# A gate in two TensorE passes: 2E copied by ScalarE, the difference taken by VectorE, the sum by POOL

## The chip, the cores and the metric

One core of one Trainium2 chip. The metric is the device time of one launch in microseconds; lower is better. A run of a kernel is several executions, of which one is recorded by the hardware profiler.

## The reference, cut to what matters

The real part of a two-dimensional Fourier transform over eight batches of 3008 x 256, and behind it a feed-forward layer with a gelu gate.

```python
def _attn_ref(x):                      # x: (8, 3008, 256)
    X = np.fft.fft(x, axis=1)
    X = np.fft.fft(X, axis=2)
    return X.real.astype(np.float32)

def _moe_ref(x, w_gate, w_val, w_out): # x: (24064, 256), d_ff = 1536
    g = x @ w_gate
    inv_sqrt2 = np.float32(1.0 / np.sqrt(2.0))
    gelu = 0.5 * g * (1.0 + erf(g * inv_sqrt2))
    val = x @ w_val
    return (gelu * val @ w_out).astype(np.float32)
```

## The kernel before

The transform of a real input is symmetric, so the kernel makes an even part E and an odd part O of the tokens and gets two tokens from each column: a token and its mirror. A batch is worked off in 36 blocks of 128 hidden units by 512, 512 or 481 columns (three chunks of twelve blocks). The text calls a block's place in the batch its slot, 0 to 35. `psum` gives banks of PSUM, into which all matmuls of this kernel write: two for the gate, three for the value, one for the output (ps_o) and two for the Fourier matmuls ("gate bank", "value bank" and "output bank" below).

```python
    def gelu_tile():
        return work([128, 2, TOK], BF16, "gelu", 5, "gelu_sb")
    def ve_tile():
        return work([128, TOK], FP32, "ve", 3, "ve_sb")
    def v_tile():
        return work([128, TOK], FP32, "v", 4, "v_sb")
    def psum(tag):
        bufs = {"g": 2, "v": 3, "o": 1, "dft": 2}[tag]
        return psum_pool.tile([128, 512], FP32, tag=tag, bufs=bufs, name=f"ps_{tag}")
```

The gate of a block is an E pass and an O pass into one bank, a gelu, then (one slot later) a pass with the weights -2O into the same bank and a second gelu for the mirror tokens. The value needs two passes only, because VectorE and POOL make the mirror:

```python
        def l1_gate(ci, fc):
            def run():
                n, _, E, O, st, fs = cols_of(ci, fc)
                pg = psum("g")
                mm(pg, n, "g", "E", fs, E, True, False)
                mm(pg, n, "g", "O", fs, O, False, True)
                gl = gelu_tile()
                nc.scalar.activation(gl[:, 0, :n], pg[:, :n], AF.Gelu)          # L676
                st["ps"][fc] = [pg, gl]
            return run
        def l1_gate2(ci, fc):
            def run():
                n, _, _, O, st, fs = cols_of(ci, fc)
                pg, gl = st["ps"][fc][:2]
                mm(pg, n, "g", "M", fs, O, False, True, skip_group_check=True)  # -2O
                nc.scalar.activation(_sub(gl, [[-1, n]], TOK + n - 1), pg[:, :n], AF.Gelu)  # L685
            return run
        # ... l1_value: E pass, then on VectorE
                nc.vector.scalar_tensor_tensor(                                 # L704
                    ve[:, :n], EB_bufs[b][:, c0 : c0 + n], yw[:, fc : fc + 1], pv[:, :n],
                    op0=ALU.mult, op1=ALU.add)
        # ... l1_value2: O pass, then
                nc.vector.tensor_tensor(st["h"][:, fc, 0, :n], gl[:, 0, :n], pv[:, :n], op=ALU.mult)   # L720
                vv = v_tile()
                nc.vector.scalar_tensor_tensor(                                 # L722
                    _sub(vv, [[-1, n]], n - 1), ve[:, :n], 2.0, pv[:, :n], op0=ALU.mult, op1=ALU.subtract)
                nc.gpsimd.tensor_tensor(st["h"][:, fc, 1, :n], gl[:, 1, :n], vv[:, :n], op=ALU.mult)   # L724
```

The changed kernel is called after below. POOL's folds are the sums and differences from which the next batch's E and O are made. In one slot the order is:

```python
            parts["G"][fc]()                      # gate of this block
            if before:
                before[0]["g"][before[1]]()       # -2O pass and second gelu of the block before
            parts["V"][fc]()                      # value E pass
            if len(two) == 2:
                two.pop(0)()                      # four output matmuls (L749)
            for f in pool.pop(i, []):
                f()                               # POOL's folds for the next batch
            if before:
                before[0]["v"][before[1]]()       # value O pass and products of the block before
            if two:
                two.pop(0)()                      # four output matmuls; some slots end with the copy of ps_o (L769)
            for f in fill.pop(i, []):
                f()                               # Fourier matmuls for the next batch
```

Of the kernel before, what the change touches and what calls it, by code (L numbers as in the profile page):

```python
# [9 lines left out]
FP32 = mybir.dt.float32  # L10
BF16 = mybir.dt.bfloat16
AF = mybir.ActivationFunctionType
ALU = mybir.AluOpType
# [5 lines left out]
def _sub(base: bass.AP, free_pattern, free_offset, part_start=0, part_num=None):  # L19
    p_step, p_count = base.ap[0]  # L20
    if part_num is None:
        part_num = p_count - part_start
    pat = [[p_step, part_num]] + [list(x) for x in free_pattern]
    off = base.offset + part_start * p_step + free_offset
    return ap_replace(base, ap=pat, offset=off)
# [3 lines left out]
def kernel(  # L29
# [8 lines left out]
    nc = tc.nc  # L38
# [5 lines left out]
    B, T, C = x.shape  # L44
# [6 lines left out]
    NFC = F // 128  # L51
# [33 lines left out]
    def work(shape, dt, tag, bufs, name):  # L85
        return work_pool.tile(shape, dt, tag=tag, bufs=bufs, name=name)
# [41 lines left out]
    def gelu_tile():  # L128
        return work([128, 2, TOK], BF16, "gelu", 5, "gelu_sb")
# [4 lines left out]
    def v_tile():  # L134
        return work([128, TOK], FP32, "v", 4, "v_sb")

    def osb_tile():
        return work([128, 2, C], FP32, "osb", 3, "out_sb")

# [3 lines that stand above are left out]
# [100 lines left out]
    keep2 = const_pool.tile([128, 1], FP32)  # L243
    dump = const_pool.tile([1, 1], FP32)
    one_h = const_pool.tile([1, 1], BF16)
    yw = const_pool.tile([128, NFC], FP32)
    NGP = NJ * NK
    ff = work([128, 2 * NGP], FP32, "EO", 2, "ff")
    rr = work([128, 2 * NGP], FP32, "EO", 2, "rr")
# [218 lines left out]
    def make_yw(f0, n):  # L468
# [7 lines left out]
            nc.scalar.activation(yw[:, c0 : c0 + nq], ps[:, 0:nq], AF.Copy)  # L476
        return run


    EO_bufs, EB_bufs = {}, {}  # L480
    turn = [0]
# [152 lines left out]
        return tp_e(b, gi, 1, engine)  # L634


    def store(b, gi, sub, sign, osb_half, queue):
        segs = [c for c in cols[gi] if c[0] // 128 == sub]
        m = min(128, chunk_len[gi] - sub * 128)
        for i, (off, k2, w) in enumerate(segs):  # L640
            p0 = off - sub * 128
            lo, hi = (1, w - 1) if sign and k2 == 0 else (0, w)
            if sign:
                t0 = T - k2 - N2 * (hi - 1)
                p1 = m - p0 - hi
            else:
                t0 = k2 + N2 * lo
                p1 = p0 + lo
            dst = ap_replace(
                out,  # L650
                ap=[[N2 * C, hi - lo], [1, C]],
                offset=out.offset + (b * T + t0) * C,
            )
            (nc.sync if i else queue).dma_start(out=dst, in_=_sub(osb_half, [[1, C]], 0, part_start=p1, part_num=hi - lo))

    def ffn_work(b):
        cstate = {}

        def mm(ps, n, nm, part, fs, src, start, stop, **kw):
            nc.tensor.matmul(ps[:, :n], W[nm, part][:, fs], src, start=start, stop=stop, **kw)  # L660

        def cols_of(ci, fc):
# [3 lines left out]
                cstate[ci] = {"h": h_tile(), "ps": {}, "pso": {}}  # L666
            return n, c0, E, O, cstate[ci], slice(fc * 128, (fc + 1) * 128)

        def l1_gate(ci, fc):
            def run():  # L670
                n, _, E, O, st, fs = cols_of(ci, fc)
                pg = psum("g")
                mm(pg, n, "g", "E", fs, E, True, False)
                mm(pg, n, "g", "O", fs, O, False, True)
                gl = gelu_tile()
                nc.scalar.activation(gl[:, 0, :n], pg[:, :n], AF.Gelu)  # L676
                st["ps"][fc] = [pg, gl]
            return run

        def l1_gate2(ci, fc):  # L680
            def run():
                n, _, _, O, st, fs = cols_of(ci, fc)
                pg, gl = st["ps"][fc][:2]
                mm(pg, n, "g", "M", fs, O, False, True, skip_group_check=True)
                nc.scalar.activation(_sub(gl, [[-1, n]], TOK + n - 1), pg[:, :n], AF.Gelu)  # L685
            return run
# [88 lines left out]
        for ci in range(NG):  # L775
            nsub = (chunk_len[ci] + 127) // 128
            parts = {k: [f(ci, fc) for fc in range(NFC)] for k, f in (
                ("G", l1_gate), ("V", l1_value), ("g", l1_gate2), ("v", l1_value2))}
            subs = [nsub - 1, *range(nsub - 1)] if last(ci) else range(nsub)
            l2s = [l2_piece(ci, s, g, f) for s in subs for g in range(2) for f in range(0, NFC, L2P)]  # L780
            chunks.append((parts, l2s))
# [91 lines left out]
        make_yw(0, 256)()  # L873
        tp_y(0, 0)()

    NS = NG * NFC

    def plan():

        fill, pool = {}, {}  # L880
# [1 line left out]
        def at(table, s, f):  # L882
            table.setdefault(s, []).append(f)
# [4 lines left out]
        for s, f in (  # L888
                (0, make_w(0, 256, 256)), (0, make_w(1, 256, 256, engine="V")), (1, make_yw(256, 256)),
                (1, make_w(1, 512, 512, (1,))), (2, make_w(0, 512, 512, (0,), "V")), (2, make_yw(512, 512)),  # L890
                (3, make_w(0, 512, 512, (1,))), (3, make_w(1, 512, 512, (0,), "V")),
                (4, make_w(1, 1024, 512, (1,), "V")), (5, make_w(0, 1024, 512, (0,), "V")), (5, make_yw(1024, 512)),
                (6, make_w(0, 1024, 512, (1,))), (7, make_w(1, 1024, 512, (0,), "V"))):
            at(fill, s, f)
        for i, f in enumerate(early):
            at(fill, (7, 8, 9, 10, 11, 12, 13, 14, 15, 16)[i], f)

# [50 lines left out]
    def feed():  # L948
        blocks, works = [], []
        for b in range(B):  # L950
            for parts, l2s in ffn_work(b):
                works.append(l2s)
                blocks += [(parts, fc) for fc in range(NFC)]
        fill, pool = plan()
        pend, before = [], None

        first = works[0]
        sooner = {8: [first[0]], 9: [first[3]], 10: [first[1]], 11: [first[4]], 13: [first[2]], 14: [first[5]]}
        works[0] = first[6:]
        for i, (parts, fc) in enumerate(blocks):  # L960
            if fc == 0 and i:
                assert not pend
                pend = list(works[i // NFC - 1])
            two = sooner.pop(i, []) if i <= NFC + 2 else [pend.pop(0) for _ in range(2) if pend]
            parts["G"][fc]()
            if i == 0:
                behind_first_gate()
            if before:
                before[0]["g"][before[1]]()
            parts["V"][fc]()  # L970
            if len(two) == 2:
                two.pop(0)()
            for f in pool.pop(i, []):
                f()
            if before:
                before[0]["v"][before[1]]()
            if two:
                two.pop(0)()
            for f in fill.pop(i, []):
                f()  # L980
            before = parts, fc
        assert not fill and not pool
        before[0]["g"][before[1]]()
        before[0]["v"][before[1]]()
        for u in works[-1]:
            u()
# [33 lines left out]
```

## Time and profile before

| before | value |
|---|---|
| median of the first three executions | 628.93 us (628.3 to 629.76) |
| span of the profiled execution | 627.0 us, mean granted clock 0.996 |
| busy: TensorE, VectorE, POOL, ScalarE | 612.3, 578.3, 505.3, 428.4 us |
| one batch in mid-run | 73.92 us |

The busy times say which engine has work for nearly the whole span: TensorE.

### The profile page before, as it was taken

How to read it: one execution, taken by the hardware profiler on the slowest of the kernel's cores; microseconds unless marked ns; L12 is line 12 of the kernel's file. 1: busy time of each engine (PE TensorE's matmuls, PEld its weight loads, DVE VectorE, ACT ScalarE, POOL GpSimd, SP SyncE). 2: the span in 40 equal slices, each digit the busy share in tenths (PEclk: the TensorE clock that was granted, in tenths of full speed). 3: DMA queues.
4: the chain of work that ended last, by engine and by line, in shares of the span. 5: the costliest groups of instructions: out<-in, count | busy, mean ns of one | idle time of the engine just before them, and what ended most of it. 6: DMA issues, size and time to landing. Idle time of an engine off the chain costs nothing.

```text
span 627.0 us, 12895 instructions
## 1 busy us (share of the span) xinstructions
PE 612.3 (98%) x4195; PEld 405.1 (65%) x4243; DVE 578.3 (92%) x941; ACT 428.4 (68%) x842; POOL 505.3 (81%) x510
## 2 busy tenths in 40 slices
PE   7999999999999999999999999999999999999997
PEld 3456666666666666666666666666666666666666
DVE  8689989999899999999999998999999999999992
ACT  6777677666776677667676677676676666666661
POOL 8399999989897998879997899969988655555651
PEclk8999999999999999999999999999999999999999
DMA  9961754536353353731645335633212322221123
GB/s 177 227 97 31 210 129 116 144 105 159 99 146 101 98 133 79 184 113 46 160 110 135 101 78 127 148 97 98 62 49 63 91 86 55 51 52 39 42 51 81
DMA packets 54217, 65.40 MB, mean 104 GB/s; under 512 B 7831, under 2 KB 49802, under 8 KB 51754
## 3 DMA queue, kind: packets, MB, share of 16 engines
q1 hardware_dynamic: 47222, 49.03, 30.6%
q0 software_dynamic: 6608, 15.29, 11.4%
q8 instruction: 33, 0.54, 0.4%
q10 hardware_dynamic: 320, 0.26, 0.2%
q14 instruction: 34, 0.28, 0.2%
HBM read 39.65 MB, written 30.17 MB: 111 GB/s over the span
## 4 chain that ended last, share of the span: by engine, by line
PE 93%; ACT 2%; issue 1%; DVE 1%; DMA 1%; POOL 1%; POOLq 0%; ACTq 0%
PE ps_o L749 38%; PE ps_g L660 28%; PE ps_v L660 19%; PE ps_dft L546 2%; PE ps_dft L582 2%; PE ps_o L820 1%; DMA Z_sb<-z 1%; PE ps_dft L443 1%; PE ps_dft L612 0%; ACT gelu_sb L676 0%; POOL h_sb L724 0%; POOL eo_sb L224 0%; DMA out_dram<-out_sb 0%; ACT gelu_sb L685 0%; PE ps_dft L749 0%
## 5 line engine op out<-in xcount | busy, mean ns | idle before, releaser
L724 POOL TENSOR_TENSOR h_sb<-gelu_sb,v_sb 128x512 bf16<-128x512 bf16 (+1 forms) x280 | 319.8, 1146 | 93.1 <-DVE v_sb L722 85.9
L749 PE MATMUL ps_o<-Wo_sb,h_sb 128*128 128x256 bf16 (+1 forms) x2232 | 334.9, 273 | 0.9 <-POOL h_sb L724 0.9
L749 PEld LDWEIGHTS <-h_sb 128*128 128x128 bf16 (+1 forms) x2304 | 228.7, 100 | 112.9 <-POOL h_sb L724 2.6
L676 ACT ACTIVATE gelu_sb<-ps_g 128x512 bf16<-128x512 f32 (+1 forms) x288 | 169.4, 588 | 98.6 <-PE ps_g L660 80.9
L660 PE MATMUL ps_g<-EO_sb,W_sb 128*128 128x512 bf16 (+1 forms) x817 | 228.5, 375 | 3.8 <-ACT gelu_sb L685 0.8
L704 DVE SCALAR_TENSOR_TENSOR ve_sb<-EB_sb,yw,ps_v 128x512 f32<-128x512 bf16 (+1 forms) x280 | 206.3, 737 | 25.9 <-PE ps_v L660 25.0
L660 PE MATMUL ps_v<-EO_sb,W_sb 128*128 128x512 bf16 (+1 forms) x575 | 213.7, 375 | 0.7 <-DVE W_sb L451 0.6
L720 DVE TENSOR_TENSOR h_sb<-gelu_sb,ps_v 128x512 bf16<-128x512 bf16 (+1 forms) x280 | 189.9, 678 | 1.1 <-ACT gelu_sb L685 0.7
L660 PEld LDWEIGHTS <-W_sb 128*128 128x128 bf16 x1440 | 137.2, 98 | 81.1 <-issue 1.8
L722 DVE SCALAR_TENSOR_TENSOR v_sb<-ve_sb,ps_v 128x512 f32<-128x512 f32 (+1 forms) x280 | 187.5, 670 | 0.0
L685 ACT ACTIVATE gelu_sb<-ps_g 128x512 bf16<-128x512 f32 (+1 forms) x288 | 168.7, 586 | 0.0
L769 ACT ACTIVATE out_sb<-ps_o 128x512 f32<-128x512 f32 x92 | 55.0, 598 | 35.7 <-PE ps_o L749 35.6
L224 POOL TENSOR_TENSOR eo_sb<-ab_sb 94x512 bf16<-94x512 f32 (+1 forms) x70 | 77.6, 1111 | 0.5
L549 ACT ACTIVATE S_sb<-ps_dft 96x512 bf16<-96x512 f32 x56 | 32.9, 588 | 14.0 <-PE ps_dft L546 13.9
L592 ACT ACTIVATE EO_sb<-ps_dft 128x512 bf16<-128x512 f32 (+1 forms) x44 | 26.0, 590 | 23.3 <-PE ps_dft L582 22.1
L217 POOL TENSOR_TENSOR ab_sb<-x_raw,x_raw 94x508 f32<-94x508 f32 (+1 forms) x30 | 33.0, 1100 | 0.0
L220 POOL TENSOR_TENSOR ab_sb<-x_raw,x_raw 94x508 f32<-94x508 f32 (+1 forms) x30 | 32.9, 1098 | 0.0
L546 PE MATMUL ps_dft<-eo_sb,G 94*96 94x256 bf16 x119 | 22.5, 274 | 0.2 <-POOL eo_sb L224 0.2
L158 POOL DMA_INDIRECT x_raw<-in_x_dram,idx x18 | 17.1, 948 | 2.9 <-issue 1.1
L582 PE MATMUL ps_dft<-TP,Z_sb 128*128 128x128 bf16 (+1 forms) x184 | 17.8, 218 | 0.0
L582 PEld LDWEIGHTS <-Z_sb 128*128 128x128 bf16 x192 | 14.6, 98 | 1.8 <-DVE Z_sb L534 0.6
L546 PEld LDWEIGHTS <-G 94*96 94x96 bf16 x119 | 13.0, 123 | 1.2 <-issue 0.4
(148 smaller groups left out, 166.2 us busy)
## 6 DMA issues: line engine op xcount, KB each, us to landing
out_dram<-out_sb SPq DMA_DIRECT2D x364, 64.0 KB
x_raw<-in_x_dram SPq DMA_DIRECT2D x10, 768.0 KB
Z_sb<-z SPq DMA_DIRECT2D x7, 768.0 KB
z<-S_sb SPq DMA_DIRECT2D x7, 576.0 KB
EB_sb<-yrow SPq DMA_DIRECT2D x14, 128.0 KB
z<-S_sb SPq DMA_DIRECT2D x7, 192.0 KB
x_raw<-in_x_dram SPq DMA_DIRECT2D x2, 640.0 KB
EB_sb<-yrow SPq DMA_DIRECT2D x7, 120.2 KB
```

Source lines behind the costliest of these rows:

```text
L224: eng.tensor_tensor(_sub(eo, [[C, nj], [1, 128]], j0 * C + g * 128), ab(0, 0, [[1, 128]]), ab(1, 0, [[1, 128]]), op=op)
L546: nc.tensor.matmul(ps[:96, q * C : (q + 1) * C], G[:, j, :], _sub(eo, [[1, C]], j * C), start=(j == js[0]), stop=(j == js[-1]))
L582: nc.tensor.matmul(ps[:, o : o + n], st["Z"][:, pair, g * 128 : g * 128 + 128], _sub(TP, [[1, n]], g * 128), start=True, stop=True)
L660: nc.tensor.matmul(ps[:, :n], W[nm, part][:, fs], src, start=start, stop=stop, **kw)
L676: nc.scalar.activation(gl[:, 0, :n], pg[:, :n], AF.Gelu)
L685: nc.scalar.activation(_sub(gl, [[-1, n]], TOK + n - 1), pg[:, :n], AF.Gelu)
L704: nc.vector.scalar_tensor_tensor(ve[:, :n], EB_bufs[b][:, c0 : c0 + n], yw[:, fc : fc + 1], pv[:, :n], op0=ALU.mult, op1=ALU.add)
L720: nc.vector.tensor_tensor(st["h"][:, fc, 0, :n], gl[:, 0, :n], pv[:, :n], op=ALU.mult)
L722: nc.vector.scalar_tensor_tensor(_sub(vv, [[-1, n]], n - 1), ve[:, :n], 2.0, pv[:, :n], op0=ALU.mult, op1=ALU.subtract)
L724: nc.gpsimd.tensor_tensor(st["h"][:, fc, 1, :n], gl[:, 1, :n], vv[:, :n], op=ALU.mult)
L749: nc.tensor.matmul(pso[:m, half], st["h"][:, fc, sign, h0 : h0 + m], Wo_sb[:, fc, :], start=(fc == 0 and not (first and sign)), stop=(fc = ...
L769: nc.scalar.activation(_sub(osb, [[1, 2 * C]], 0, part_num=m), pso[:m, :], AF.Copy)
```

## The change

Its intent is to take one TensorE pass from the gate of three blocks a batch, as the value has it already. ScalarE copies 2E out of the bank after the E pass, VectorE makes d = (mirror term) - (E + O), and POOL makes 2E + d, which is the argument of the second gelu. It is done in slots 4, 28 and 33 of batches 1 to 6, so in 18 of 288 blocks. VectorE's difference is emitted ahead of the first gelu of the same bank. The core of the diff (declarations and the once-only `make_ywg`, which fills `ywg` in slot 14 of batch 0, are left out):

```diff
+    GATE2 = (4, 28, 33)
+        def two_gate(ci, fc):
+            return 0 < b < B - 1 and ci * NFC + fc in GATE2
         def l1_gate(ci, fc):
             def run():
                 n, _, E, O, st, fs = cols_of(ci, fc)
                 pg = psum("g")
+                if two_gate(ci, fc):
+                    mm(pg, n, "g", "E", fs, E, True, True)
+                    e2 = e2_tile()
+                    nc.scalar.activation(e2[:, :n], pg[:, :n], AF.Copy, scale=2.0)
+                    st["ps"][fc] = [pg, gelu_tile(), e2]
+                    return
...
+        def l1_gate_odd(ci, fc):
+            def run():
+                if not two_gate(ci, fc):
+                    return
+                n, c0, _, O, st, fs = cols_of(ci, fc)
+                pg, gl, e2 = st["ps"][fc][:3]
+                del st["ps"][fc][2]
+                mm(pg, n, "g", "O", fs, O, False, True, skip_group_check=True)
+                d = v_tile()
+                nc.vector.scalar_tensor_tensor(
+                    d[:, :n], EB_bufs[b][:, c0 : c0 + n], ywg[:, fc : fc + 1], pg[:, :n],
+                    op0=ALU.mult, op1=ALU.subtract)
+                nc.scalar.activation(gl[:, 0, :n], pg[:, :n], AF.Gelu)
+                nc.gpsimd.tensor_tensor(d[:, :n], e2[:, :n], d[:, :n], op=ALU.add)
+                st["ps"][fc][0] = d
+            return run
         def l1_gate2(ci, fc):
...
+                if two_gate(ci, fc):
+                    nc.scalar.activation(_sub(gl, [[-1, n]], TOK + n - 1), pg[:, :n], AF.Gelu)
+                    return
                 mm(pg, n, "g", "M", fs, O, False, True, skip_group_check=True)
...
             if len(two) == 2:
                 two.pop(0)()
+            parts["O"][fc]()
             for f in pool.pop(i, []):
                 f()
```

In the changed kernel the lines have moved: the copy of 2E is L696, the regular first and second gelu L702 and L731, the difference L715, the first gelu of a changed block L718, the sum L719, its second gelu L728, the products L766 and L770, the output matmul L795, the copy of ps_o L815, the gate and value matmuls L677.

More of the change, by code (lines that the diff above doesn't have):

```diff
@@ L135, in v_tile, with e2_tile @@
         return work([128, TOK], FP32, "v", 4, "v_sb")
+    def e2_tile():
+        return work([128, TOK], FP32, "e2", 1, "e2_sb")
     def osb_tile():
@@ L245 @@
     one_h = const_pool.tile([1, 1], BF16)
-    yw = const_pool.tile([128, NFC], FP32)
+    yw, ywg = (const_pool.tile([128, NFC], FP32, name=f"yw_{i}") for i in "vg")
     NGP = NJ * NK
@@ L477, in make_yw, with make_ywg @@
         return run
+    def make_ywg():
+        fcs = sorted({i % NFC for i in GATE2})
+        ps = psum("dft")
+        for fc in fcs:
+            nc.tensor.matmul(
+                ps[:, fc : fc + 1], W["g", "O"][0:1, fc * 128 : (fc + 1) * 128], one_h, start=True, stop=True)
+        for fc in fcs:
+            nc.scalar.activation(ywg[:, fc : fc + 1], ps[:, fc : fc + 1], AF.Copy, scale=2.0)
     EO_bufs, EB_bufs = {}, {}
@@ L634, in tp_o @@
         return tp_e(b, gi, 1, engine)
+    NS = NG * NFC
+    GATE2 = (4, 28, 33)
     def store(b, gi, sub, sign, osb_half, queue):
@@ L777, in ffn_work @@
             parts = {k: [f(ci, fc) for fc in range(NFC)] for k, f in (
-                ("G", l1_gate), ("V", l1_value), ("g", l1_gate2), ("v", l1_value2))}
+                ("G", l1_gate), ("O", l1_gate_odd), ("V", l1_value), ("g", l1_gate2), ("v", l1_value2))}
             subs = [nsub - 1, *range(nsub - 1)] if last(ci) else range(nsub)
@@ L874, in behind_first_gate @@
         tp_y(0, 0)()
-    NS = NG * NFC
     def plan():
@@ L894, in plan @@
             at(fill, s, f)
+        at(fill, 14, make_ywg)
         for i, f in enumerate(early):
```

## The prediction

> **What bounds the kernel now.** I number the batches 0 to 7 and the 36 feed-forward blocks of a batch 0 to 35 ("slots"). I read the page's busy times and the chain that ended last first, then one batch in the view by windows.
>
> ```profile
> PE 612.3 (98%) x4195; PEld 405.1 (65%) x4243; DVE 578.3 (92%) x941; ACT 428.4 (68%) x842; POOL 505.3 (81%) x510
> PE 93%; ACT 2%; issue 1%; DVE 1%; DMA 1%; POOL 1%; POOLq 0%; ACTq 0%
> 331.00:408.00 77.00, 76.62 (x527) 51.12 (x532) 73.16 (x113) 54.27 (x106) 67.77 (x67) 1.00 0.45 114
> ```
>
> TensorE is the bound: 76.62 of 77.00 us in mid-run, at full clock. VectorE has 3.8 us free in that window, POOL 9.2, ScalarE 22.7. The averages do not show how tightly the small buffers couple them. The timeline of ScalarE and TensorE around slots 4 to 6 of batch 4 does (start, duration, engine, line):
>
> ```profile
> 329.47 0.60 ACT L676 ACTIVATE gelu_sb<-ps_g 128x512 bf16<-128x512 f32 x1 [0.87 <-PE ps_g L660]
> 331.16 0.59 ACT L549 ACTIVATE S_sb<-ps_dft 96x512 bf16<-96x512 f32 x1 [0.60 <-PE ps_dft L546]
> 332.14 0.59 ACT L685 ACTIVATE gelu_sb<-ps_g 128x512 bf16<-128x512 f32 x1
> 333.11 0.60 ACT L769 ACTIVATE out_sb<-ps_o 128x512 f32<-128x512 f32 x1 [0.38 <-PE ps_o L749]
> 328.78 0.81 PE L660 MATMUL ps_g<-EO_sb,W_sb 128*128 128x512 bf16 x3
> 334.00 0.60 PE L749 MATMUL ps_o<-Wo_sb,h_sb 128*128 128x256 bf16 x4
> ```
>
> Slot 4 starts at 328.78. ps_o has one bank, so the output matmuls of slot 6 (334.00) need the copy L769 of slot 5 done; it ends at 333.71. So only about 0.24 us of room is left after a handover of 0.05 (the second gelus that TensorE waits for, at 46.02 and 162.18 us, end 0.05 before its start).
>
> [...] 0.65 us for the three before the value matmul at 329.43, so 0.217 each; 0.203 at 481 columns. [...] every one of its instructions starts in program order, 0.45 to 0.49 us apart when full. [...] the trace has 1.17 for the product L724, and 1.26 for a 508-element fp32 sum.
>
> **The change part by part.** In batches 1 to 6, slots 4, 28 and 33, 18 blocks.
> *Removed:* the pass with -2O in the next slot. 6 x (0.217 + 2 x 0.203) = 3.7 us of TensorE, all of it on the bound. The odd pass only moves, behind the value matmul and four output matmuls.
> *VectorE:* 18 more operations like L704 on a PSUM bank, 0.72 us from start to start: 13 us, 2.1 per batch. With TensorE 0.6 shorter, the 3.8 us free in the window shrink to about 1.1. VectorE does not become the bound by the sum, and TensorE has 1.4 us before a value bank is missing, against a lag of 0.7. I put this at nothing.
> *ScalarE:* 18 copies of 2E; it has room. *POOL:* 18 fp32 sums of about 1.25 us.
> *Once:* two one-column matmuls and two tiny copies in batch 0, 0.2 us.
>
> The new waits are what I count.
>
> (1) The odd pass must wait for the copy of 2E. Counted from the slot's start, TensorE is ready for it after E, -2O of the block before, value E and four output matmuls: 3 x 0.217 + 0.44 = 1.09 us (1.05 at 481). In slot 4 the copy starts at 0.47, takes 0.60, hands over in 0.05: 1.12, a wait of 0.03. In slot 33 an output copy of slot 32 stands before it:
>
> ```profile
> 388.65 0.60 ACT L769 ACTIVATE out_sb<-ps_o 128x512 f32<-128x512 f32 x1 [0.39 <-PE ps_o L749]
> 389.14 0.57 ACT L676 ACTIVATE gelu_sb<-ps_g 128x481 bf16<-128x481 f32 x1
> 388.45 0.78 PE L660 MATMUL ps_g<-EO_sb,W_sb 128*128 128x481 bf16 x3
> ```
>
> The slot starts at 388.45, ScalarE is free at 389.14, the copy ends near 389.71, the odd pass can start at 389.76 and could have at 389.50: 0.26 us lost where 0.20 is gained. Slot 28 has an EO copy (L592) before it in batches 2 to 6 and the same numbers. Sum: 6 x 0.26 + 5 x 0.26 + 0.03 + 5 x 0.03 + 0.25 (slot 4 of batch 1, which also has a copy ahead) = 3.3 us. This alone eats the gain.
>
> (2) The second gelu of the block waits for POOL's sum, which waits for VectorE, and all later ScalarE work stands behind it. Slot 4 of batch 4: VectorE's L704 starts at 329.85, the difference runs from 330.57 to 331.32, the first gelu starts at 331.37 instead of 329.47, then the S copy at 331.86, the gelu of slot 5 at 332.34. POOL:
>
> ```profile
> 330.65 1.15 POOL L724 TENSOR_TENSOR h_sb<-gelu_sb,v_sb 128x512 bf16<-128x512 bf16 x1
> 332.00 1.17 POOL L724 TENSOR_TENSOR h_sb<-gelu_sb,v_sb 128x512 bf16<-128x512 bf16 x1 [0.20 <-DVE v_sb L722]
> ```
>
> It is free at 331.80, so the sum ends at 333.05, the second gelu starts at 333.10 instead of 332.14, and the ps_o copy at 333.59 instead of 333.11; the bank is free at 334.24. TensorE, 0.18 ahead of before, wants it at 333.82: 0.42 lost. The queue behind (S copy, two gelus) frees the gate bank for slot 7 at 335.68, wanted at 335.33: 0.35 more. Batches 3 to 5 alike, 0.77 each; batch 1 0.3 and batch 6 0.5, where POOL is free sooner; batch 2 about 2.3, since POOL is 2 us behind there (two products from 184.17 with 2.28 us of busy time, the sum between them). Together 5.4 us. Slot 28 has the same form with a ps_o copy at 29; there POOL is free when VectorE is done and I find 0 to 0.1 at the output bank and some 0.27 at the gate bank of slot 31: 1.5 us over the batches. Slot 33 has no output copy at 34: nothing.
>
> (3) POOL at the end of a batch. In batches 2 to 4 its last product already ends when TensorE needs it:
>
> ```profile
> 399.45 2.24 POOL L724 TENSOR_TENSOR h_sb<-gelu_sb,v_sb 128x481 bf16<-128x481 bf16 x2
> 400.21 0.71 PE L749 MATMUL ps_o<-Wo_sb,h_sb 128*128 128x256 bf16 x4
> ```
>
> The first of the two products ends near 400.55, and the four output matmuls take 0.71 us instead of 0.60, so the last one waits for it. The sum of slot 33, less 0.52 us of POOL's idle time there, comes out about 0.6 later: 3 x 0.6 = 1.8 us.
>
> Sum: -3.7 + 3.3 + 5.4 + 1.5 + 1.8 + 0.2 = +8.5 us. The waits are not independent: a TensorE that was held once arrives later at the next and waits less, and VectorE and POOL catch up meanwhile. I choose to keep about two thirds, +5.5 us: 628.9 + 5.5 = 634.5.
>
> **The rivals.** (a) The waits are hidden and only the matmuls count: 628.9 - 3.7 + 0.2 = 625.4. For it: TensorE is 99% busy in mid-run, and the three slots were evidently chosen where extra Fourier matmuls give VectorE slack (its idle 0.17 to 0.47 us before L704 sits in slots 5, 6, 28 to 30 and 34). Against: ScalarE is a strict queue, and the free 0.24 us of the ps_o bank and 0.05 of the gate bank are no room for a second gelu that comes 1 us late. (b) VectorE becomes the bound. Over a batch its work rises from 73.2 to 75.3 us against about 76: it would be idle almost nowhere, and any lag that piles up past 1.4 us would hold TensorE at the value banks. Against: it spreads over 36 slots and TensorE's own waits give it time. It would make 629 to 632. (c) The waits add up in full, and POOL's lag, which grows by some 3.75 us of work in 9.2 free, also delays the folds that the Fourier matmuls need: 637 to 641.
>
> **Range and chances.** (a) at about 1 in 7, (c) at about 1 in 6, the rest between: 627.5 to 641 for 8 in 10. 2% is 12.6 us. To be that much faster would take more than three times the removed matmul time; to be that much slower, half as much again as my full sum. So faster 0.01, same 0.95, slower 0.04.
>
> **What would show it.** Right: waits of TensorE on ps_g for the new copy, near 0.26 us each, in slots 28 and 33; waits of ps_o on the output copy at slot 6 (0.1 to 0.8, most in batch 2); an idle ScalarE before the second gelu of these blocks, put down to POOL; gate matmuls 18 fewer; a batch 0.2 to 3 us longer, not 0.6 shorter. VectorE busy near 591 us. Wrong: if the output copy of slot 5 still starts within 0.2 us after its matmuls, step (2) falls and with it most of the loss; if TensorE waits mostly for ps_v, rival (b) is right; if mid-run batches get shorter by 0.6 us, rival (a).

Measured in the trace of before: three matmuls of 512 columns (0.65 us), then the instructions of ScalarE (all 840 start in program order), then POOL's durations. Why the first gelu has to stand behind VectorE's read of the same bank was not shown; that it does stand there is measured in after, where the first gelu L718 waited for the difference L715 in all 18 places, 15.4 us in sum. The 1.4 us before a value bank is missing are an estimate; before supports them: around slot 4 of batch 4, L722 ends 1.90 us or more before the L704 three slots later, and from the value matmul to its L704 it is 0.42 us (329.43 to 329.85), so some 1.4 are left after a handover of 0.05.

## The result

| | before | after |
|---|---|---|
| median of four executions each, same rounds | 629.35 us (628.3 to 630.05) | 639.33 us (639.15 to 639.75) |
| ratio | | 1.0161, 95% interval 1.0143 to 1.0179 |
| span of the profiled execution | 627.0 us | 637.9 us |

The ratios in this document are the mean time of one kernel's runs over that of the other's of the same rounds, so they are not quite the ratio of the medians quoted beside them. The change made the kernel 10 us slower, inside the 2% that counts as the same.

The page of the profile after: busy times with instruction counts, and the chain that ended last.

```profile
PE 617.0 (97%) x4227; PEld 404.1 (63%) x4227; DVE 585.2 (92%) x959; ACT 436.3 (68%) x862; POOL 525.5 (82%) x528
PE 79%; POOL 8%; ACT 5%; DMA 3%; issue 2%; DVE 2%; SPq 0%; POOLq 0%; ACTq 0%; DVEq 0%
```

The view by windows of after, in the same stretch of mid-run (length, then busy time of TensorE, weight loads, VectorE, ScalarE and POOL, then clock and DMA):

```profile
331.00:408.00 77.00, 75.52 (x521) 49.89 (x519) 73.14 (x114) 53.69 (x106) 70.00 (x70) 1.00 0.45 112
```

TensorE lost 14 points of the chain, to POOL, ScalarE, DMA and VectorE, and in mid-run it now stands idle for 1.48 of 77 us instead of 0.38. VectorE is busy for 92% of the span in both, so the busy times do not make it the new bound. Its 18 new operations took 13.1 us in sum; the busy time rose by 6.9 only, because it counts stretches in which two operations overlap once (all durations of VectorE sum to 621.4 us before and 634.1 after). (TensorE's busy total of after isn't less than before: matmul ends are modelled, and a part of this execution ran at a lower clock, see below.) The output matmuls tell it best, in the pages' table of groups (busy us, mean ns, then idle time just before them and what ended most of it). Before:

```profile
L749 PE MATMUL ps_o<-Wo_sb,h_sb 128*128 128x256 bf16 (+1 forms) x2232 | 334.9, 273 | 0.9 <-POOL h_sb L724 0.9
```

After:

```profile
L795 PE MATMUL ps_o<-Wo_sb,h_sb 128*128 128x256 bf16 (+1 forms) x2232 | 335.4, 273 | 7.0 <-ACT out_sb L815 3.7
```

The same matmuls cost the same, but TensorE stood idle 7.0 us before them instead of 0.9, over half of it for ScalarE's copy of ps_o. The view of waits of after (total us, times, longest us) names the chain behind it:

```profile
ACT gelu_sb L718 <- DVE v_sb L715: 15.4, 18, 1.0
...
ACT gelu_sb L728 <- POOL v_sb L719: 4.4, 6, 2.4
PE ps_o L795 <- ACT out_sb L815: 3.7, 5, 2.2
...
PE ps_o L795 <- POOL h_sb L770: 2.8, 4, 0.8
```

**Where it was lost.** I compared the two traces slot by slot, from the start of one value E matmul to the next. All numbers are after minus before, in us. "Slot" is where the comparison shows it, which can be one slot before or after the block that causes it.

| batch | length before | change | of it: removed passes (3, 27, 32) | slot 6 | slot 28 | slot 33 | slot 2 (batch boundary) |
|---|---|---|---|---|---|---|---|
| 1 | 75.70 | +0.82 | -0.62 | +0.21 (and +0.22 in slot 4) | 0 | +0.23 | 0 |
| 2 | 74.03 | +5.05 | -0.63 | +3.88 | +1.23 | +0.23 | 0 |
| 3 | 73.92 | +1.64 | -0.62 | +0.66 | +0.26 | +0.23 | +0.92 |
| 4 | 73.92 | +1.63 | -0.62 | +0.68 | +0.26 | +0.23 | +0.91 |
| 5 | 73.93 | +1.60 | -0.62 | +0.66 | +0.26 | +0.23 | +0.90 |
| 6 | 72.91 | +0.64 | -0.63 | +0.51 | +0.26 | +0.23 | 0 |

Batch 0 was 0.70 shorter, the opening 0.29 longer, batch 7 the same. Smaller changes are left out of the table; the largest of them are +0.51 in slot 30 and +0.27 in slot 10 of batch 1. Three places explain nearly all of the loss in batches 3 to 6.

*The odd pass waits for the copy of 2E.* Slot 33 of batch 4 in the timeline of after (start, duration, engine, line):

```profile
397.28 0.60 ACT L815 ACTIVATE out_sb<-ps_o 128x512 f32<-128x512 f32 x1 [0.39 <-PE ps_o L795]
397.77 0.57 ACT L696 ACTIVATE e_sb<-ps_g 128x481 f32<-128x481 f32 x1
...
398.39 0.36 PE L677 MATMUL ps_g<-EO_sb,W_sb 128*128 128x481 bf16 x1
```

The slot starts at 397.08 and the odd pass at 398.39, 1.31 later. The prediction had worked out exactly that: 389.76 - 388.45 = 1.31.

*The second gelu comes late, and the copy of ps_o behind it.* Slots 4 to 6 of batch 4, which start at 336.78 in after:

```profile
339.25 0.60 ACT L718 ACTIVATE gelu_sb<-ps_g 128x512 bf16<-128x512 f32 x1 [0.97 <-DVE v_sb L715]
...
339.77 1.26 POOL L719 TENSOR_TENSOR v_sb<-e_sb,v_sb 128x512 f32<-128x512 f32 x1
...
341.06 0.63 ACT L728 ACTIVATE gelu_sb<-v_sb 128x512 bf16<-128x512 f32 x1 [0.25 <-POOL v_sb L719]
...
341.60 0.58 ACT L815 ACTIVATE out_sb<-ps_o 128x512 f32<-128x512 f32 x1
...
342.23 0.60 PE L795 MATMUL ps_o<-Wo_sb,h_sb 128*128 128x256 bf16 x4 [0.28 <-ACT out_sb L815]
...
343.67 0.59 PE L677 MATMUL ps_g<-EO_sb,W_sb 128*128 128x512 bf16 x2 [0.20 <-ACT gelu_sb L731]
```

Read it downwards: POOL's sum ends at 341.03, the second gelu starts at 341.06, the copy of the output bank at 341.60, and TensorE, idle for 0.28 us, starts as that copy has ended. (Idle time counts from the modelled end of the matmul before, at 341.94; the next could have started at 341.78, one 512-column pass of 0.217 us after that one's start at 341.56, so 0.45 us were lost there.) Counted from the slot's start these are 4.25, 4.28, 4.82 and 5.45 us; the prediction had 4.27, 4.32, 4.81 and 5.46.

*POOL's last product of a batch comes late.* The end of batch 4, on POOL and TensorE:

```profile
407.85 1.30 POOL L227 TENSOR_TENSOR eo_sb<-ab_sb 94x512 bf16<-94x512 f32 x1
409.09 2.23 POOL L770 TENSOR_TENSOR h_sb<-gelu_sb,v_sb 128x481 bf16<-128x481 bf16 x2
...
410.26 0.28 PE L795 MATMUL ps_o<-Wo_sb,h_sb 128*128 128x256 bf16 x1 [0.84 <-POOL h_sb L770]
```

The chunk's last block needs its product before the fourth output matmul of the next chunk can run; a fold (L227) stands before it. In batch 2, where POOL is two microseconds behind, the second place is much dearer:

```profile
187.35 0.63 ACT L728 ACTIVATE gelu_sb<-v_sb 128x512 bf16<-128x512 f32 x1 [2.43 <-POOL v_sb L719]
...
188.52 0.69 PE L795 MATMUL ps_o<-Wo_sb,h_sb 128*128 128x256 bf16 x4 [2.21 <-ACT out_sb L815]
...
190.71 1.48 PE L677 MATMUL ps_g<-EO_sb,W_sb 128*128 128x512 bf16 x3
```

TensorE stood still for 2.21 us, and then three gate matmuls took 1.48 us from first start to last end instead of 0.81. The view by windows says why (the column before the last two is the granted clock):

```profile
186.00:188.00 2.00, 0.31 (x2) 0.03 (x1) 1.51 (x3) 0.65 (x2) 2.00 (x3) 1.00 0.02 5
188.00:190.00 2.00, 1.48 (x8) 0.97 (x8) 0.26 (x1) 1.91 (x4) 2.00 (x4) 0.72 0.14 32
190.00:192.00 2.00, 2.00 (x9) 1.00 (x8) 1.03 (x2) 0.73 (x2) 1.35 (x3) 0.50 0.44 99
192.00:194.00 2.00, 2.00 (x14) 1.31 (x13) 1.43 (x3) 0.95 (x2) 0.33 (x1) 0.93 0.84 217
```

After the stall the clock was 0.50 for 3.41 us, from 188.89 to 192.30, and I put about 1.5 us of this batch's loss to it (an estimate: of slot 6's +3.88 the stall takes 2.21, and the 3.1 us of the slot that ran at half clock would take half as long at full clock). That holds for the profiled execution only. The four executions had mean clocks of 0.993, 0.996, 0.997 and 1.000 and took 639.75, 639.15, 639.27 and 639.39 us, so the one with no lowered clock in its records was not faster. What it lost instead isn't recorded.

### The profile page after: what moved, and what is told of

The parts are those of the page before. It is cut to its first block, busy times and chain, and to the rows that moved or that the text cites. A ratio compares the mean times of both kernels' runs of the same rounds, so it can differ in the third digit from the quotient of the medians.

```text
span 637.9 us, 12969 instructions
## 1 busy us (share of the span) xinstructions
PE 617.0 (97%) x4227; PEld 404.1 (63%) x4227; DVE 585.2 (92%) x959; ACT 436.3 (68%) x862; POOL 525.5 (82%) x528
## 4 chain that ended last, share of the span: by engine, by line
PE 79%; POOL 8%; ACT 5%; DMA 3%; issue 2%; DVE 2%; SPq 0%; POOLq 0%; ACTq 0%; DVEq 0%
PE ps_o L795 32%; PE ps_g L677 24%; PE ps_v L677 16%; POOL h_sb L770 3%; PE ps_dft L559 2%; DMA out_dram<-out_sb 2%; PE ps_dft L595 1%; ACT out_sb L815 1%; POOL ab_sb L223 1%; ACT gelu_sb L702 1%; POOL eo_sb L227 1%; DMA EO_sb<-yrow 1%; ACT gelu_sb L731 1%; DVE ve_sb L750 1%; ACT EO_sb L605 1%
## 5 line engine op out<-in xcount | busy, mean ns | idle before, releaser
L770 POOL TENSOR_TENSOR h_sb<-gelu_sb,v_sb 128x512 bf16<-128x512 bf16 (+1 forms) x280 | 318.7, 1144 | 79.5 <-DVE v_sb L768 73.6
L795 PE MATMUL ps_o<-Wo_sb,h_sb 128*128 128x256 bf16 (+1 forms) x2232 | 335.4, 273 | 7.0 <-ACT out_sb L815 3.7
L795 PEld LDWEIGHTS <-h_sb 128*128 128x128 bf16 (+1 forms) x2304 | 229.0, 100 | 123.2 <-issue 8.6
L677 PE MATMUL ps_g<-EO_sb,W_sb 128*128 128x512 bf16 (+1 forms) x846 | 230.8, 376 | 3.5 <-ACT gelu_sb L731 1.3
L750 DVE SCALAR_TENSOR_TENSOR ve_sb<-EB_sb,yw_v,ps_v 128x512 f32<-128x512 bf16 (+1 forms) x280 | 206.1, 736 | 23.2 <-PE ps_v L677 21.6
L702 ACT ACTIVATE gelu_sb<-ps_g 128x512 bf16<-128x512 f32 (+1 forms) x270 | 159.1, 589 | 90.9 <-PE ps_g L677 83.5
L677 PE MATMUL ps_v<-EO_sb,W_sb 128*128 128x512 bf16 (+1 forms) x576 | 214.3, 376 | 0.7 <-DVE W_sb L454 0.6
L766 DVE TENSOR_TENSOR h_sb<-gelu_sb,ps_v 128x512 bf16<-128x512 bf16 (+1 forms) x280 | 189.6, 677 | 4.4 <-PE ps_v L677 2.2
L677 PEld LDWEIGHTS <-W_sb 128*128 128x128 bf16 x1422 | 135.6, 98 | 82.1 <-issue 6.6
L731 ACT ACTIVATE gelu_sb<-ps_g 128x512 bf16<-128x512 f32 (+1 forms) x270 | 158.5, 587 | 0.0
L227 POOL TENSOR_TENSOR eo_sb<-ab_sb 94x512 bf16<-94x512 f32 (+1 forms) x70 | 77.6, 1110 | 0.5
L815 ACT ACTIVATE out_sb<-ps_o 128x512 f32<-128x512 f32 x92 | 54.8, 596 | 32.4 <-PE ps_o L795 32.4
L719 POOL TENSOR_TENSOR v_sb<-e_sb,v_sb 128x481 f32<-128x481 f32 (+1 forms) x18 | 22.0, 1225 | 4.5 <-DVE v_sb L715 4.5
L718 ACT ACTIVATE gelu_sb<-ps_g 128x481 bf16<-128x481 f32 (+1 forms) x18 | 10.5, 582 | 15.4 <-DVE v_sb L715 15.4
```

The lines of the kernel that those rows point to most:

```text
L227: eng.tensor_tensor(_sub(eo, [[C, nj], [1, 128]], j0 * C + g * 128), ab(0, 0, [[1, 128]]), ab(1, 0, [[1, 128]]), op=op)
L677: nc.tensor.matmul(ps[:, :n], W[nm, part][:, fs], src, start=start, stop=stop, **kw)
L750: nc.vector.scalar_tensor_tensor(ve[:, :n], EB_bufs[b][:, c0 : c0 + n], yw[:, fc : fc + 1], pv[:, :n], op0=ALU.mult, op1=ALU.add)
L795: nc.tensor.matmul(pso[:m, half], st["h"][:, fc, sign, h0 : h0 + m], Wo_sb[:, fc, :], start=(fc == 0 and not (first and sign)), stop=(fc = ...
L815: nc.scalar.activation(_sub(osb, [[1, 2 * C]], 0, part_num=m), pso[:m, :], AF.Copy)
```

## The experiments

My theory: the three waits above cost what they cost in the timeline, and they add up in full. The rivals were that they are partly hidden by each other (what the prediction had assumed), and that VectorE is near its limit and would be the bound if the waits were gone. The kernel before was run beside each group; its medians in the four groups were 629.66, 630.49, 630.01 and 629.79 us. All kernels gave a correct result but one, which is named.

### One slot at a time: slot4, slot28, slot33

```diff
-    GATE2 = (4, 28, 33)
+    GATE2 = (4,)          # slot4;  (28,) in slot28;  (33,) in slot33
```

> Only slot 4 of each of the six batches is changed (6 blocks instead of 18). Theory (waits behind ScalarE and POOL): the costs of the slots add. From the changed kernel's own trace, slots 4 to 7 gained 0.22 us of matmul per batch and lost 0.43, 4.04, 0.66, 0.68, 0.66 and 0.51 us in batches 1 to 6; so about +5.5 us against the kernel before, of which some 4 in batch 2, with the output matmuls of slot 6 waiting for the output copy of slot 5. No wait at the batch ends. Rival (VectorE's extra work is the cost): 0.7 us a batch fit into VectorE's free 3.8 us a batch, so the time falls by about 1.3 us. Rival (POOL's extra work at the batch end is the cost): slot 4 is far from the end, also -1.3 us.

> Only slot 28 of each of the six batches. Theory: wait of the odd pass for the copy of 2E, 0.26 us in batches 3 to 6 and about 1.2 in batch 2 (an EO copy that waits for a transfer stands before it on ScalarE), some 0.1 to 0.5 at slot 30, less 0.20 of matmul in each: about +2 us. Rival (VectorE): about -1.2 us. No wait at the batch ends, since POOL has caught up by slot 33.

> Only slot 33 of each of the six batches. Theory: 0.23 us at the odd pass and 0.06 at the output copy of slot 35 against 0.20 of matmul, six times, and 0.9 us at slot 2 of batches 3, 4 and 5, where TensorE waits for POOL's last product of the batch before: about +3 us. If the wait at the batch end needs the sums of slots 28 and 33 together, it is smaller and the total about +1. Rival (VectorE): -1.2 us.

| run | median | ratio to before | by median | where (after minus before, us) |
|---|---|---|---|---|
| slot4 | 635.66 us | 1.0092 (1.0065 to 1.0119) | +6.0 | slot 3 -0.22, slot 6 +0.64 to +0.66 in batches 3 to 5; batch 2 +4.91, of which slot 28, where nothing is changed, has +1.10 |
| slot28 | 631.65 us | 1.0029 (1.0011 to 1.0048) | +2.0 | slot 27 -0.20, slot 28 +0.26, slot 30 +0.12 to +0.14; batch 1 slot 30 +0.53 |
| slot33 | 633.35 us | 1.0047 (1.0023 to 1.0071) | +3.7 | slot 32 -0.20, slot 33 +0.23, slot 2 of batches 3 to 5 +0.90 |

Expected were +5.5, +2 and +3. By their ratios (times 629.7 us) the three cost 5.8, 1.8 and 3.0 us, together 10.6, with an uncertainty of some 2.6 from the three intervals; all three in one kernel cost 10.0. The traces say it more sharply: in batches 3, 4 and 5 the three single changes add to +1.65, +1.66 and +1.58 us, and the full change has +1.64, +1.63 and +1.60. There the waits add up. (In batch 6 it is +0.30 beside +0.64, so together they cost more; batches 1 and 2 are blurred by transfers.) Each wait appears in the slots where the theory puts it, and slot 4 of batch 2 alone is some 3.8 us of everything. That refutes the assumption of the prediction that a TensorE held once waits less afterwards.

One piece of batch 2 does not belong to the change: its slot 28 lost 0.75 in slot33 and 1.10 in slot4, which change nothing there, and 0.55 in before_product_first (below). In slot33 it is ScalarE that waits there, 1.42 us at 232.17, for a transfer into EO_sb whose landing moves from run to run: the wait is 0.51 us in before (at 230.59) and 1.29 in after (at 235.61).

### Without POOL's sum: no_sum (wrong result, relative error 0.205)

```diff
                 nc.scalar.activation(gl[:, 0, :n], pg[:, :n], AF.Gelu)
-                nc.gpsimd.tensor_tensor(d[:, :n], e2[:, :n], d[:, :n], op=ALU.add)
                 st["ps"][fc][0] = d
```

> The changed kernel without POOL's sum: the second gelu reads the difference before 2E is added, so the result is wrong on purpose. VectorE's and ScalarE's extra work stay. Theory: the waits for POOL go (batch ends 3 x 0.9 us, most of slot 6 of batch 2), those of the odd pass for the copy stay (0.23 to 0.26 us, slots 28 and 33), and at slots 6 and 7 some 0.5 us a batch stay, since ScalarE still starts its queue 1.9 us late behind VectorE: +3 to +4 us against the kernel before instead of +10. Rival (VectorE is the bound): still about +10 us.

Measured: 632.43 us, ratio 1.0042 (1.0021 to 1.0063), about +2.6 us, near the lower end of what was expected. The waits at the batch boundaries are gone (slot 2: -0.04), the stall of batch 2 in slot 6 is gone, slot 6 of batches 3, 5 and 6 lost 0.32 to 0.33 instead of 0.51 to 0.66 (in batch 4 it was 0.68 and slot 30 0.47, for which I have no reason), and the copy waits of slots 28 and 33 stay at 0.26 and 0.23. So of the 10 us, some 7.4 hang on POOL's sum (this run takes it away; the next ones move it), and what is left is the copy of 2E and VectorE's difference ahead of the gelu, less the removed passes.

### The sum on VectorE: sum_dve

```diff
-                nc.gpsimd.tensor_tensor(d[:, :n], e2[:, :n], d[:, :n], op=ALU.add)
+                nc.vector.tensor_tensor(d[:, :n], e2[:, :n], d[:, :n], op=ALU.add)
```

> The changed kernel with its sum on VectorE in place of POOL, right behind the difference: 11 to 13 us more of VectorE, POOL as before the change. Theory (VectorE's work is not what costs): close to the run without the sum, +3 to +5 us against the kernel before, the batch-end wait gone; VectorE's free time in a batch (3.8 us less 2.1, 1.9 and what TensorE gains) is about used up, so a little may come on top. Rival (VectorE is the bound): above the changed kernel, +15 us or more.

Measured: 638.97 us, ratio 1.0131 (1.0109 to 1.0154), about +8.3 us: more than expected. The timelines of this run show why. VectorE, batch 2:

```profile
185.60 2.83 DVE L719 TENSOR_TENSOR v_sb<-e_sb,v_sb 128x512 f32<-128x512 f32 x1
```

POOL at the same time:

```profile
185.48 1.27 POOL L227 TENSOR_TENSOR eo_sb<-ab_sb 94x512 bf16<-94x512 f32 x1
186.71 1.16 POOL L770 TENSOR_TENSOR h_sb<-gelu_sb,v_sb 128x512 bf16<-128x512 bf16 x1
```

TensorE, held for a value bank:

```profile
189.68 0.38 PE L677 MATMUL ps_v<-EO_sb,W_sb 128*128 128x512 bf16 x1 [1.84 <-DVE v_sb L768]
```

The sum took 0.66 us in slots 28 and 33 of batch 6, where POOL ran nothing beside it, and 0.78 to 2.83 us elsewhere, 1.02 in the median of all 18. (The 11 to 13 us expected were an estimate; VectorE's two-input operations of 508 elements take 0.68 us in before, which makes 12.2 for 18. Measured were 21.7.) At 185.60 it ended 0.56 us after POOL's second instruction. Each of the 16 sums that began beside a POOL instruction ended 0.51 to 0.56 us after the end of one (the one at 109.37 took 1.50 us and ended at 110.87, 0.55 after POOL's at 110.32). In 4 of the 16, the one at 185.60 among them, the sum ended only after a POOL instruction that had started after it (here at 186.71, 1.11 us later). So the run does not show VectorE's limit for one more plain instruction, as I had meant it to; it shows that this two-input sum from SBUF is a bad guest on VectorE beside a busy POOL. The difference L715 of the change has one SBUF tensor and one PSUM operand, and took 0.72 to 0.75 us in all 18 places of after, beside POOL or not, as its like L750 does (0.71 to 0.75).

### Odd pass and second gelu later: moved

The odd pass, the first gelu (now ahead of the difference), the difference and the sum go behind the second group of output matmuls of the slot, and the second gelu with its product one slot further on. The emission order, cut to what matters:

```diff
             if len(two) == 2:
                 two.pop(0)()
-            parts["O"][fc]()
...
             if two:
                 two.pop(0)()
+            parts["O"][fc]()
...
+            if before2:
+                before2[0]["L"][before2[1]]()     # second gelu and its POOL product, two slots late
             parts["V"][fc]()
```

> Same three slots, same instructions, another order: the odd pass, the first gelu, the difference and the sum stand behind the slot's last output matmuls (so the copy of 2E has a whole slot and the gelu needs no VectorE result), and the second gelu with the product that reads it comes one slot later, behind the other gelus. Theory (waits behind ScalarE): the waits at the odd pass (slots 28 and 33) and at slots 6, 7 and 30 go, the one for POOL at the batch ends (3 x 0.9 us) stays: -0.5 to +1 us against the kernel before instead of +10. Rival (VectorE's extra work is the cost): its work is the same, so still +5 us or more, with waits at the value banks.

Measured: 636.62 us, ratio 1.010 (1.0079 to 1.012): missed by 5 us. In batches 3 to 6 the losses of slots 6, 28 and 30 are gone, so the theory was right on those; 0.20 to 0.21 us remain in slot 33, where TensorE, ahead by the missing pass, waits for the output copy of slot 32. But slot 33 is near the batch's end, and its late second gelu now stands ahead of the last copy of ps_o. ScalarE at the end of batch 3:

```profile
324.90 0.60 ACT L781 ACTIVATE gelu_sb<-v_sb 128x481 bf16<-128x481 f32 x1 [0.88 <-POOL v_sb L719]
325.41 0.58 ACT L827 ACTIVATE out_sb<-ps_o 128x512 f32<-128x512 f32 x1
```

TensorE there:

```profile
326.04 0.60 PE L807 MATMUL ps_o<-Wo_sb,h_sb 128*128 128x256 bf16 x4 [0.82 <-ACT out_sb L827]
...
331.73 0.28 PE L807 MATMUL ps_o<-Wo_sb,h_sb 128*128 128x256 bf16 x1 [0.65 <-POOL h_sb L772]
```

It is the same wait as in slot 6 of the change, at another place: +0.83 to +1.01 us in slot 0 of batches 2 to 6, and POOL's +0.72 in slot 2 of batches 3 to 5. Another +1.21 is in slot 7 of batch 2, where the second gelu waited 1.25 us for POOL's sum. The order was mended; the place was not.

### Other slots: moved_4_19_28

```diff
-    GATE2 = (4, 28, 33)
+    GATE2 = (4, 19, 28)      # on top of moved
```

> The run above with slot 33 exchanged for slot 19, so that no sum falls into the last blocks of a batch. Theory: the wait at the batch ends goes as well; what is left is 18 passes less, -3.7 us, and 0.3 to 0.6 us for the two small columns in batch 0: about -3 us, a kernel faster than both. Rival (VectorE): no difference to the run above.

Measured: 632.6 us, ratio 1.0036 (1.0014 to 1.0058): missed by some 5 us. In batch 6, which has no folds to do, the whole saving arrives: 72.28 instead of 72.91 us, -0.64, for three passes of about 0.21. In batches 3 to 5 little is lost within the batch either (0.2 us in slot 31 of two of them), and no value bank is waited for: VectorE has room for three more operations a batch. But all that TensorE gains it gives back in slot 2 of the next batch, +1.06 to +1.10 us. POOL and TensorE at the end of batch 3:

```profile
328.36 1.29 POOL L227 TENSOR_TENSOR eo_sb<-ab_sb 94x512 bf16<-94x512 f32 x1
329.58 2.23 POOL L772 TENSOR_TENSOR h_sb<-gelu_sb,v_sb 128x481 bf16<-128x481 bf16 x2
...
330.76 0.28 PE L807 MATMUL ps_o<-Wo_sb,h_sb 128*128 128x256 bf16 x1 [1.01 <-POOL h_sb L772]
```

My reading, which the next runs test: POOL paces the end of these batches. A TensorE that comes sooner by 0.64 us waits longer by as much, and the three sums add to it.

### The last product of a chunk ahead of the fold: before_product_first, moved_product_first, moved_product_first2

```diff
-            for f in pool.pop(i, []):
+            folds = pool.pop(i, [])
+            if fc == 0 and before:
+                before[0]["v"][before[1]]()
+            for f in folds:
                 f()
-            if before:
+            if fc and before:
                 before[0]["v"][before[1]]()
```

The first is the kernel before with this edit alone, as a control. The second is moved_4_19_28 with it. The third also leaves out slot 4 of batch 2 and fills `ywg` in slot 24 instead of 14.

> The kernel before, with one thing changed: in the first slot of each chunk POOL does the last product of the chunk before ahead of the fold that stands there, not behind it. Control for the two runs beside it. Theory: the kernel before loses about 0.1 us at the end of batches 2 to 4 to this product, so nothing measurable: 0 to -0.5 us.

> The reordered version with slots 4, 19 and 28, and POOL's last product of a chunk ahead of the fold in the next chunk's first slot. Theory (at the batch end POOL, not TensorE, sets the pace, so what TensorE gains in a batch is given back there): the waits of 1.06 to 1.10 us at slot 2 of batches 3 to 5 go, and these batches get 0.65 us shorter than before, as batch 6 did in the run without this change; in all -2 to -3 us against the kernel before instead of +2. Rival (something else holds TensorE at slot 2, VectorE's lag for one): the wait stays or turns up at another instruction, and the time stays near +2.

> As the run above, without slot 4 of batch 2 (POOL is 2 us behind there and the wait at slot 7 was 0.8 us), and with the two small columns made in slot 24 of batch 0, not 14. Theory: about 0.7 us better in batch 2 than the run above where that wait stays, and up to 0.5 us in batch 0: -3 to -4 us against the kernel before.

| run | median | ratio to before | batches 3, 4, 5, 6 | batch 0 and batch 1 |
|---|---|---|---|---|
| before_product_first | 629.48 us | 1.000 (0.9973 to 1.0027) | -0.10, -0.09, -0.11, 0 | -1.71, -0.01 |
| moved_product_first | 632.3 us | 1.0008 (0.9975 to 1.0041) | -0.29, -0.44, -0.64, -0.64 | +0.83, +3.74 |
| moved_product_first2 | 630.65 us | 1.0008 (0.9985 to 1.0032) | -0.26, -0.33, -0.69, -0.64 | +3.30, +3.33 |

The wait at the batch boundary is gone, and batches 3 to 6 are now all shorter than before: POOL's order was the cause. By itself the edit gives 0.1 us a batch, too little to see in the time. As totals both expectations were missed, by the profiled executions through batches 0 and 1 (that of moved_product_first2 was the slowest of its seven, 634.03 us, and lost 2.8 us of batch 0 in a wait for a weight transfer). ScalarE in batch 1 of moved_product_first:

```profile
163.48 0.60 ACT L605 ACTIVATE EO_sb<-ps_dft 128x512 bf16<-128x512 f32 x1 [2.66 <-DMA EO_sb<-yrow]
```

A copy into EO_sb waited 2.66 us for a transfer of one row into the same buffer, and TensorE lost 3.7 us in slots 30 and 31 behind it: it stood idle for 1.61, 0.26 and 0.54 us, and then the clock was 0.50 from 166.27 to 169.68, to which most of the rest can be put. It happens in the profiled executions of both kernels with the early batches changed. Of the six executions of moved_product_first four took 632.3 us and two 628.0 and 628.8, so it probably does not happen in every one, but the two were not traced. The same copy waits for the same transfer in other runs too, but for 0.36 to 1.06 us (1.06 in late_batches below, whose batch 1 is unchanged). Whether the faster TensorE makes the wait so long or the transfer comes late by itself is not separated, and it stays open.

### Only the batches where it pays: late_batches, late_batches4

```diff
         def two_gate(ci, fc):
-            return 0 < b < B - 1 and ci * NFC + fc in GATE2
+            return 2 < b < B - 1 and ci * NFC + fc in GATE2   # on top of moved_product_first
...
-        at(fill, 14, make_ywg)
+        at(fill, 24, make_ywg)
```

GATE2 is (4, 19, 28) in late_batches and (4, 12, 19, 28) in late_batches4.

> The reordered version (slots 4, 19, 28, last product of a chunk ahead of the fold, columns made in slot 24 of batch 0) in batches 3 to 6 alone: 12 passes less. Batches 1 and 2, where transfers and POOL are behind, stay as before. Theory: batches 3 to 6 get 0.3, 0.4, 0.65 and 0.65 us shorter, the rest is that of the control: -2 us against the kernel before, a ratio near 0.997. Rival (the run-to-run spread of the transfers in batches 0 to 2 is larger than the gain): no measurable difference.

> As the run above with a fourth slot, 12, in each of the four batches: 16 passes less. VectorE's 3.8 free us of a batch less 4 x 0.72 and 4 x 0.2 leave some 0.1. If VectorE's limit lies where this sum puts it: no gain over the run above, and TensorE waits at the value banks or for products turn up (0 to +1 us on top of the run above). If only waits behind ScalarE and POOL count: another 0.2 us a batch better, -3 us in all.

late_batches: 628.21 us (627.89 to 628.57) beside 629.79 of before, ratio 0.9971 (0.9946 to 0.9996). Batches 3 to 6 changed by -0.47, -0.44, -0.64 and -0.64, together -2.2 us, where twelve removed passes come to about -2.5. It is the only version here that beats the kernel before, and by 0.3%, well inside what counts as the same. The same place as in moved_4_19_28, end of batch 3, on POOL and TensorE:

```profile
326.10 1.14 POOL L772 TENSOR_TENSOR h_sb<-gelu_sb,v_sb 128x481 bf16<-128x481 bf16 x1
327.17 1.29 POOL L227 TENSOR_TENSOR eo_sb<-ab_sb 94x512 bf16<-94x512 f32 x1
...
328.96 0.60 PE L807 MATMUL ps_o<-Wo_sb,h_sb 128*128 128x256 bf16 x4
```

The product now runs ahead of the fold, and the four output matmuls run unbroken in 0.60 us.

late_batches4: 631.93 us, ratio 1.0032 (1.0003 to 1.0061). The fourth slot saves its 0.22 in slot 11, but the batches changed by +0.41, +0.59, -0.17 and -0.79. What was lost, in slot 22 (+0.63 in batches 3 to 5) and slot 26 (+0.47 in batches 3 and 4), is again POOL. ScalarE, batch 3:

```profile
294.40 0.63 ACT L781 ACTIVATE gelu_sb<-v_sb 128x512 bf16<-128x512 f32 x1 [0.85 <-POOL v_sb L719]
```

The sum of slot 19 came late, its gelu held ScalarE, and TensorE waited 0.47 us for a gate bank at 296.54. No value bank was waited for. So the limit that a fourth block meets in this place (no other was tried) is POOL's lag beside the folds, not VectorE, and batch 6 without folds gains again (-0.79). The change by batches is 2.2 us worse than in late_batches; in the profiled executions the rest of the difference lies in the opening and the early batches, where batch 0 alone moved by -1.7 to +3.3 us among the runs shown here.

## Why the prediction was right or wrong

Predicted were 634.5 us, range 627.5 to 641; measured 639.33. The range held it, the middle was 4.8 us too low. The range reached from no loss at all to above the full sum, so that it held the result says little; the terms say more.

- **TensorE is the bound, and the removed passes are all on it.** Right: -0.22, -0.20 and -0.20 in the three slots. As worked out, -3.7 us. The weight loads of gate and value, which the records hold in full, fell from 1440 to 1422; of the matmul records some are missing, so their counts in the pages don't show it.
- **(1) The odd pass waits for the copy.** Right: 3.3 us predicted; measured 0.23 in slot 33, 0.26 in slot 28 of batches 3 to 6, 0.22 in slot 4 of batch 1, together 2.6. The +1.23 in slot 28 of batch 2 comes on top, but 0.55 to 1.10 of that is there in runs that don't change that slot.
- **(2) The second gelu waits for POOL and holds ScalarE's queue.** Right as a mechanism, to within 0.05 us in each step of the timeline. (A full ScalarE starts its instructions of 512 columns up to 0.495 us apart in before, and in after the copy at 341.60 started 0.54 after the second gelu at 341.06; so it is not 0.49 at most. Nothing hangs on it.) In size, slot 6 of batches 3 to 5 was 0.66 to 0.68 instead of 0.77, because the working left out that the kernel before already loses 0.12 us at the gate bank of slot 7 (its matmuls start at 335.21; the output matmuls ahead of them were through at 335.09); batch 6 was 0.51 as predicted; slot 30 was 0.11 to 0.13 in most batches instead of 0.27, but 0.51 in batch 1. Batch 2 was the large miss: 2.3 us for slot 6 predicted, 3.88 measured in the profiled execution, of which 2.21 is one stall at the output bank, the size that I had worked out (though the signs I listed put at most 0.8 of it at that bank), and the rest mostly the halved clock that I had not thought of.
- **(3) POOL at the batch's end.** Right in place, three boundaries and no more, and too small: 0.6 us each predicted, 0.90 to 0.92 measured. The working took POOL's idle 0.52 us off the cost of the sum, but not that POOL would stand idle anew before it: it waits 0.34 us for the difference (its sum starts at 399.73 in batch 4).
- **VectorE's 13 us cost nothing.** Right: the 18 differences took 13.1 us in sum, and TensorE did not wait for value banks. (The busy time, 585.2 us and not 591, is smaller because overlaps count once.) moved_4_19_28 shows room for three more operations a batch, late_batches4 for four.
- **The once-only copies.** 0.2 us predicted, 0.58 measured in slot 14 of batch 0, where the bank of the Fourier matmuls is held for them. That batch 0 is shorter in total is not their doing: slots 17, 26 and 27 gained 1.26, but before_product_first, which has no such copies, gained 1.69 in the same slots.
- **"The waits are not independent ... I choose to keep about two thirds."** This is the step that failed. The sum of the working was +8.5 us, and the choice cut it to +5.5. slot4, slot28 and slot33 cost 10.6 us apart and 10.0 together, and in batches 3 to 5 their traces add up to within 0.03 us: there nothing is shared. I take the distance between the slots to be the reason; that was not tested. Of rival (c), the full sum was the right reading; its other half, folds that come too late for the Fourier matmuls, is not in the trace (no such wait in the view of waits of after). That 8.5 lies near the 10 measured is partly luck. Term by term in the profiled execution: -3.7 removed, 2.6 for (1), some 6.3 for (2) without the halved clock (6.9 predicted), 2.7 for (3) (1.8 predicted), together 7.9. The other 3 us up to the 10.9 between the profiled executions are the halved clock (some 1.5), slot 28 of batch 2 (1.23) and small changes, none of which was foreseen.
- **The rivals.** (a) is refuted by every run with the original order. (b) is refuted for one more operation of this kind; for two it was not tested cleanly, because the second one is blocked by POOL.

Open: why the one-row transfer lands late in batch 1 of the two faster kernels, and how much of the lowered clock counts in executions that were not traced.

## What to carry to other kernels

To take work from the bound engine and give it to engines with room helps only if the new chain meets its deadline at each handover: here 3.7 us of matmuls were exchanged for a chain over four engines, whose last link stood, in ScalarE's program order, ahead of the copy that frees the only output bank (341.06 and 341.60 in slot 5 of batch 4). Ask for every added instruction what stands behind it in its queue and by when that is wanted, and add such waits in full unless the timeline shows one swallowing another. If the order and the places are chosen by these deadlines (late_batches), the same idea gains here some 2 us in the batches that it changes; the one try at a fourth block a batch lost to POOL's lag.

## What else the traces show

- The granted clock after a stall. In after it was 0.50 from 188.89 to 192.30, and in the 3.41 us before that TensorE's records leave it idle for 2.21 us, all in one stall. At the start of the kernel it was 0.50 from 11.39 to 14.81 after 2.07 us of idle time in as long a stretch (before: from 11.19 to 14.61 after 1.98). In slot4 a stall of 2.20 us ended at 189.41, and the clock was 0.64 in 190:192 and 0.51 in 192:194. In sum_dve the stall of 1.84 us that ended at 189.68 was not followed by a lower clock (1.00 in 190:192). What decides between them was not tested.
- POOL's time per instruction. The fp32 sums and folds of two inputs took 0.19 us at 2 columns, 0.44 at 127, 1.26 at 508 and 1.264 at 512 (means in after). From these I estimate about 2.1 ns per column and some 0.19 us fixed.
- The delay from the end of one engine's instruction to the start of the one on another engine that waits for it. In slots 5 and 6 of batch 4 of after the second gelu started 0.03 us after POOL's sum (341.03 to 341.06), and TensorE 0.05 us after the copy of ps_o (342.18 to 342.23).
